# Beginning the expert units behind two attention halves, with weight tiles and later halves placed unit by unit

## The chip, the cores and the metric

The kernel runs on one core of one Trainium2 chip. The metric is the device time of one execution in microseconds, the median of the runs. The engines are TensorE (PE in the rows, with PEld for its weight loads), VectorE (DVE), ScalarE (ACT), GpSimd (POOL) and SyncE (SP). SP issues nearly all transfers, in one queue. Each engine works through its own instructions in a fixed order; an instruction waits for what it needs, and all behind it on that engine wait with it.

## The reference

Three stages follow one another. The inputs are float32, but the weight matrices of both networks are 64-bit values.

```python
def _attn_ref(q, k, v, alpha):              # batch 4, 8 heads, 768 steps, head size 48
    for t in range(S):
        state = alpha[:, :, t, :, None] * state + einsum('bhd,bhe->bhde', k[:, :, t], v[:, :, t])
        y[:, :, t] = einsum('bhd,bhde->bhe', q[:, :, t], state)

def _moe_ref(x, w_in, w_out, a, b):         # 3072 tokens, 384 -> 2048 -> 384
    h = x @ w_in
    P = a[0] + a[1] * h + a[2] * h**2 + a[3] * h**3
    Q = 1.0 + abs(b[0]) * abs(h) + abs(b[1]) * h**2
    return (P / (Q + 1e-06)) @ w_out

def _moe2_ref(x, w_in, w_out, g_ln):        # 384 -> 1024 -> 384
    h = x @ w_in
    solu = h * softmax(h)
    return (layer_norm(solu) * g_ln) @ w_out
```

## The kernel before

The 768 steps are cut into six chunks of 128; a chunk over four batch elements is 512 tokens. A chunk of the attention is made in two **halves** of two batch elements each, so there are twelve halves. Halves 0 and 1 turn their inputs with PE (`a_turn`). All later ones are prepared by `a_dve`, mostly on DVE, in six steps: transposes, a forward scan (L312), a backward scan (L321), products, and two stores to device memory from which the halves come back turned (L333, L341; `a_move_qk` L280, `a_move` L286). `a_pe` then makes the scores (L424; copied by ACT L431 and masked by POOL L432), the outputs `y` (L448), which ACT and DVE write as a high and a low part into the chunk's token tile `xt` (L474, L475), and the state (L487).

The first network runs in 96 **units**: unit u is one chunk of 512 tokens times 128 of the 2048 hidden columns. `m_up` does nine matmuls (L604) into one of three `hp` banks, then a chain over ACT, DVE and, in even units below 24, POOL (L609 to L635; the last DVE operation, L628 or L635, is noted as `fin[u]`), and a split into `gh` and `gl` (L637, L638). `m_down` of the unit four back does nine matmuls (L650) into the chunk's three sums. The order of the units is written by hand: chunk 0 with its columns 0 to 11, chunk 1 with 0 to 7, chunk 0 with 12 to 15 (units 20 to 23), chunk 1 with 8 to 15, then chunks 2 to 5 whole. A chunk done in two parts stores two partial results, `x2b_d` and `x2_d`; the copies `x2e` (L659) carry them.

The weights come in four **groups** of seven tiles each (three of `w_in`, four of `w_out`). `split_w` loads a tile, makes float32 of it by three DVE operations (L541, L544, L545), and splits it in a rounded high part (ACT, L551) and the rest (POOL, L552). Where the loaded bytes wait is one of two `st` buffers or space lent by a later group's buffer; `x2e` uses `st` as well.

Before unit 0 stand, in program order, halves 0 and 1, groups 0 and 1 whole, the constants (`consts`, with two broadcast transfers, L117 and L118), and the preparation of half 2. Then the loop over units starts. In it `BEGIN` says at which unit a half's `a_pe` begins (`half_steps`, one step of `a_pe` per unit and two steps of the next half's preparation), `CONV` when groups 2 and 3 begin (one tile per unit), `LINGER` that half 4's preparation waits for unit 16, and `U2`, `IDLE` at which units a tile of the second network's weights is split (`w2_split`). `pin(n)` and `later(n)` put instructions behind those of unit u - n on the same engine; apart from that, the order on each engine is planned ahead from a model of the times, in which earlier lines of the program go first among what is ready.

The second network follows: `n_load` brings a chunk's 512 results back (for chunks 0 and 1 the two partial results are added on DVE, L695), splits them by ACT and POOL (L697, L698), and each block of 128 tokens goes through `n_up` (18 matmuls, L731), softmax and norm (`n_soft`, `n_norm`), a transposing round through SBUF transfers (`n_turn`), `n_split` and `n_down` (24 matmuls, L795). The blocks of the first chunk are worked on beside the last units; `n_load(1)` stands right behind the last unit.

## Time and profile before

| | |
|---|---|
| median of 3 runs | 794.52 us (794.39 to 795.79) |
| the profiled execution | 793.51 us, of which the instructions span 791.8 us |
| PE | busy 735.1 us, 93% of the span |
| DVE | busy 624.9 us, 79% |
| ACT | busy 540.1 us, 68% |
| POOL | busy 351.0 us, 44% |
| mean granted clock of TensorE | 0.96 of full |

Times are counted from the first instruction. A line such as L604 is a line of the kernel. An engine is busy while one of its instructions runs; the busy time of PE counts overlapping matmuls once. "idle before" is the time an engine stood before an instruction, and the name behind the arrow is what released it, as far as the profile can tell. The granted clock is the share of TensorE's full clock; it has two levels here, 0.5 (1.2 GHz) and 1.0 (2.4 GHz), so that a value between them is a mean over time.

### The profile page before, as it was taken

How to read it: one execution, taken by the hardware profiler on the slowest of the kernel's cores; microseconds unless marked ns; L12 is line 12 of the kernel's file. 1: busy time of each engine (PE TensorE's matmuls, PEld its weight loads, DVE VectorE, ACT ScalarE, POOL GpSimd, SP SyncE). 2: the span in 40 equal slices, each digit the busy share in tenths (PEclk: the TensorE clock that was granted, in tenths of full speed). 3: DMA queues.
4: the chain of work that ended last, by engine and by line, in shares of the span. 5: the costliest groups of instructions: out<-in, count | busy, mean ns of one | idle time of the engine just before them, and what ended most of it. 6: DMA issues, size and time to landing. Idle time of an engine off the chain costs nothing.

```text
span 791.8 us, 13947 instructions
## 1 busy us (share of the span) xinstructions
PE 735.1 (93%) x4976; PEld 612.2 (77%) x4976; DVE 624.9 (79%) x1116; ACT 540.1 (68%) x989; POOL 351.0 (44%) x306
## 2 busy tenths in 40 slices
...
PEclk9857899988999999999999999999999999999999
...
GB/s 175 276 249 172 69 193 2 72 135 172 182 141 204 112 218 162 139 93 203 159 121 121 151 151 1 287 172 0 2 120 146 60 141 79 139 129 47 114 109 83
DMA packets 88719, 104.90 MB, mean 132 GB/s; under 512 B 34624, under 2 KB 63296, under 8 KB 88640
## 3 DMA queue, kind: packets, MB, share of 16 engines
...
## 4 chain that ended last, share of the span: by engine, by line
PE 51%; DVE 23%; ACT 9%; DMA 7%; issue 5%; SPq 3%; POOL 2%; DVEq 0%; ACTq 0%; POOLq 0%
PE h L731 13%; PE op L795 12%; PE x2p L650 11%; PE hp L604 11%; DVE w L633 2%; PE y L448 2%; DVE p L630 2%; DVE hp L634 2%; DVE P L312 2%; PE sc L424 2%; DMA rq<-in_q_dram 2%; DVE fp L544 2%; DVE p L635 1%; SPq L270 1%; DVE fp L541 1%
## 5 line engine op out<-in xcount | busy, mean ns | idle before, releaser
L604 PE MATMUL hp<-xt,g 128*128 128x512 f32 x864 | 225.8, 403 | 9.5 <-DVE p L628 7.5
L638 POOL TENSOR_TENSOR gl<-p,gh 128x512 fp32r<-128x512 f32 x96 | 127.0, 1323 | 199.1 <-ACT gh L637 111.3
L604 PEld LDWEIGHTS hp<-xt,g 128*128 128x128 f32 x864 | 164.3, 193 | 49.4 <-DVE p L628 8.3
L650 PE MATMUL x2p<-gh,g 128*128 128x512 f32 x576 | 196.5, 397 | 1.4 <-ACT x2e L659 1.4
L650 PEld LDWEIGHTS x2p<-gh,g 128*128 128x128 f32 x576 | 108.9, 189 | 28.2 <-ACT x2e L659 3.5
L650 PE MATMUL x2p<-gl,g 128*128 128x512 f32 x288 | 114.1, 396 | 1.1 <-POOL gl L638 1.1
L795 PE MATMUL op<-w2oh,room 128*128 128x384 f32 x384 | 101.7, 339 | 0.2 <-DVE room L787 0.2
L731 PE MATMUL h<-w2ih,x 128*128 128x512 f32 x288 | 93.1, 399 | 3.0 <-ACT x L697 2.7
L787 POOL TENSOR_TENSOR room<-room,room 128x1024 fp32r<-128x1024 f32 x22 | 54.1, 2464 | 93.7 <-ACT room L786 93.6
L633 DVE SCALAR_TENSOR_TENSOR w<-w,co,hp 128x512 f32<-128x512 f32 x84 | 62.0, 738 | 41.1 <-ACT hp L632 40.4
L609 ACT ACTIVATE ah<-hp 128x512 f32<-128x512 f32 x96 | 56.9, 593 | 26.5 <-PE hp L604 25.5
L611 ACT ACTIVATE p<-hp,co 128x512 f32<-128x512 f32 x96 | 65.9, 687 | 8.3 <-POOL gl L638 8.1
L612 ACT ACTIVATE w<-ah,co 128x512 f32<-128x512 f32 x96 | 69.4, 724 | 2.8 <-DVE hp L634 2.4
L795 PEld LDWEIGHTS op<-w2oh,room 128*128 128x128 f32 x384 | 70.1, 188 | 1.4 <-DVE room L787 0.5
L630 DVE SCALAR_TENSOR_TENSOR p<-p,co,hp 128x512 f32<-128x512 f32 x84 | 61.9, 737 | 10.0 <-ACT p L611 9.6
L632 ACT ACTIVATE hp<-ah 128x512 f32<-128x512 f32 x84 | 50.3, 598 | 26.3 <-DVE p L630 25.3
L731 PEld LDWEIGHTS h<-w2ih,x 128*128 128x128 f32 x288 | 54.5, 190 | 15.7 <-ACT x L697 3.1
L650 PEld LDWEIGHTS x2p<-gl,g 128*128 128x128 f32 x288 | 54.6, 189 | 13.6 <-POOL gl L638 1.6
L795 PE MATMUL op<-w2ol,room 128*128 128x384 f32 x192 | 65.0, 339 | 0.0
L637 ACT ACTIVATE gh<-p 128x512 fp32r<-128x512 f32 x96 | 59.9, 625 | 6.8 <-PE x2p L650 4.2
L635 DVE SCALAR_TENSOR_TENSOR p<-p,co,hp 128x512 f32<-128x512 f32 x84 | 62.0, 739 | 1.2
L631 ACT ACTIVATE ah<-w,co 128x512 f32<-128x512 f32 x84 | 60.6, 721 | 1.1
...
## 6 DMA issues: line engine op xcount, KB each, us to landing
...
```

Of the source, the lines that this page charges most:

```text
L604: last["PE", u] = nc.tensor.matmul(hp, lhsT=w[:, kt, 128 * o:128 * o + 128], rhs=xts[c][:, kt, xx, :], start=(kt == 0 and w is hi and xx = ...
L611: nc.scalar.activation(p, hp, AF.Square, bias=co[:, 7:8])
L612: nc.scalar.activation(w, ah, AF.Square, bias=co[:, 6:7])
L630: nc.vector.scalar_tensor_tensor(p, p, a1, hp, ALU.add, ALU.mult)
L631: nc.scalar.activation(ah, w, AF.Ln, bias=rest)
L633: nc.vector.scalar_tensor_tensor(w, w, rest, hp, ALU.add, ALU.mult)
L635: fin[u] = nc.vector.scalar_tensor_tensor(p, p, a0, hp, ALU.add, ALU.mult)
L637: last["ACT", u] = nc.scalar.activation(gh, p, AF.Copy)
L638: last["POOL", u] = nc.gpsimd.tensor_tensor(gl, p, gh[:].bitcast(F32), ALU.subtract)
L650: nc.tensor.matmul(x2ps[c][d], lhsT=w[:, o, 128 * d:128 * d + 128], rhs=gg, start=((c, f) in first and w is hi and gg is gh), stop=((c, f) ...
L731: nc.tensor.matmul(hp[:, 512 * n:512 * n + 512], lhsT=x2s[c][:, kt, x, CH * b:CH * b + CH], rhs=w2[w][:, kt, 512 * n:512 * n + 512], start ...
L795: nc.tensor.matmul(op, lhsT=x[:, 128 * f:128 * f + 128], rhs=w2[w][:, f, :], start=(f == 0 and x is hi and w == "oh"), stop=(f == NF2 - 1 ...
```

## The change

- The preparation before unit 0 is cut to halves 0 and 1 and the three `w_in` tiles of group 0 (`PRE`). The constants come behind the loads of both halves.
- The other four tiles of group 0 and groups 1 and 2 form one chain `prep`: two tiles per unit up to unit 6, then one (`PIECES`). Group 3 begins at unit 13 as before. All of them go behind the last DVE operation of the unit before (`G1` = 1).
- Half 2's preparation is a chain `lead`, two steps in each of units 0 to 3. Half 2's `a_pe` begins at unit 4 (was 2), half 3's at 9 (was 8). `LINGER` is gone: half 4's preparation goes with half 3's `a_pe`, from unit 9 on.
- The second network's weights: the tile that was split at unit 20 is split at unit 33.
- The two score tiles of a head pair are one tile of twice the size. The partial result of unit 11 is copied into these two tiles instead of `st`.
- `TURN`: in the second network chunk 2 comes second and chunk 1 third.

```diff
--- before.py
+++ after.py
@@ -71,20 +71,20 @@
     FASTS = (0, 20)
     GE = 80
     NA = 5
-    PRE = (1, 1, 0, 0)
+    PRE = (1, 1, 1, 0)
     GP = 2
     GS = 2
-    G1 = 99
+    G1 = 1
     G2 = 3
     MIX = lambda u: u < 24 and u % 2 == 0
     EARLY = (9, 11, 13, 15)
     SKIP = (5, 7, 11)
     AHEAD = 3
-    U2, IDLE = 20, (0, NF1 // 2 - 1)
-    BEGIN = {2: 2, 8: 3, 21: 4, 27: 5}
+    U2, IDLE = 2 * NF1 - 1, (0, NF1 // 2 - 1)
+    BEGIN = {4: 2, 9: 3, 21: 4, 27: 5}
     BEGIN.update({16 * c + 2 + 8 * x: 2 * c + 2 + x for c in range(2, NCH - 1) for x in range(2)})
-    CONV = {0: 2, 13: 3}
-    LINGER = {3: 16}
+    PIECES = lambda u: 2 if u < 7 else 1
+    TURN = (0, 2, 1) + tuple(range(3, NCH))
     assert (B, H, D, CH) == (4, 8, 48, 128)
 
     const = ctx.enter_context(tc.tile_pool(name="const", bufs=1, side="left"))
@@ -426,8 +426,9 @@
                             lhsT=hf.k[p][64 * j:64 * j + D, x, :], rhs=hf.q[p][64 * j:64 * j + D, x, :],
                             start=True, stop=True,
                         )
+                both = ap_.tile([128, 2, B, CH], F32, name="A", tag=f"A{p}")
                 for j in range(2):
-                    t = A[p, j] = ap_.tile([128, B, CH], F32, name="A", tag=f"A{p}{j}")
+                    t = A[p, j] = both[:, j]
                     nc.scalar.activation(t, sc[j], AF.Copy)
                     nc.gpsimd.affine_select(
                         out=t, in_=t, pattern=[[0, B], [1, CH]], compare_op=ALU.is_ge, fill=0.0, base=0,
@@ -554,6 +555,8 @@
                 nc.sync.dma_start(out=keep, in_=both[:, :2 * n].bitcast(F32).rearrange("p (x n) -> p x n", x=2))
 
         def w1_group(n):
+            if fast:
+                stage["wide"], stage["near"] = n < 2, n == 2
             w = moe_pool.tile([128, GW], F32R, name=f"g{n}", tag=f"g{n}")
             hi, lo = (w[:, 512 * KT * x:512 * KT * (x + 1)].rearrange("p (a b) -> p a b", a=KT) for x in range(2))
             for kt in range(KT):
@@ -654,7 +657,10 @@
             if (c, f) in final:
                 to = x2_d[c] if f == NF1 - 1 else x2b_d[c]
                 for d0, n in ((0, 2), (2, 1)):
-                    e = moe_pool.tile([128, 2, NTOK], F32, name="x2e", tag="st", bufs=2)
+                    if u == 11 and fast:
+                        e = ap_.tile([128, 2, NTOK], F32, name="x2e", tag=f"A{d0 // 2}")
+                    else:
+                        e = moe_pool.tile([128, 2, NTOK], F32, name="x2e", tag="st", bufs=2)
                     for d in range(n):
                         nc.scalar.activation(e[:, d], x2ps[c][d0 + d], AF.Copy, scale=back if fast else 1.0)
                     nc.sync.dma_start(out=to[:, d0:d0 + n, :], in_=e[:, :n])
@@ -685,6 +691,7 @@
 
         def n_load(c):
             t = x2s[c] = moe_pool.tile([128, KT, 2, NTOK], F32R, name="x2", tag="xt", bufs=2)
+            c = TURN[c]
             for kt in range(KT):
                 raw = t[:, kt, 1].bitcast(F32)
                 nc.sync.dma_start(out=raw, in_=x2_d[c][:, kt, :])
@@ -800,6 +807,7 @@
 
         def n_out(s, op):
             c, qq = divmod(s, 4)
+            c = TURN[c]
             o = moe_pool.tile([128, DM], F32, name="o", tag="st", bufs=2)
             nc.scalar.activation(o, op, AF.Copy)
             to = out.rearrange("(b c q j) d -> c q b j d", b=B, c=NCH, q=4)[c, qq]
@@ -829,26 +837,18 @@
             _run(a_load(0))
             take(pre, PRE[0])
             v_load(0)
-            consts()
             take(pre, PRE[1])
             _run(a_load(1))
             take(pre, PRE[2])
             v_load(1)
             take(pre, PRE[3])
+            consts()
             nc.gpsimd.memset(Sbd, 0.0)
-            _run(a_turn(0), a_pe(0), a_turn(1), a_pe(1), pre)
+            _run(a_turn(0), a_pe(0), a_turn(1), a_pe(1))
             clear()
-            pre = w1_group(1)
-            take(pre, NA)
             _run(a_load(2, ("ra", "rk")))
-            with tc.issue_after(marks[0, 1].ins):
-                _run(a_prep(2))
-            _run(a_move_qk(2))
-            _run(a_enter(2), pre)
-            _run(a_load(3, ("ra", "rk")))
-            stage["wide"] = False
-            stage["near"] = True
-            stage["bank"] = "at"
+            prep = chain(pre, w1_group(1), w1_group(2))
+            lead = chain(a_prep(2), a_move_qk(2), a_enter(2), a_load(3, ("ra", "rk")))
         else:
             for n in range(NG):
                 _run(w1_group(n))
@@ -864,7 +864,7 @@
         def pin(n):
             stack = ExitStack()
             if n <= now[0] < NU and fast:
-                for e, u in (("PE", now[0]), ("ACT", now[0] - n), ("POOL", now[0] - n)):
+                for e, u in (("PE", now[0] - (("PE", now[0]) not in last)), ("ACT", now[0] - n), ("POOL", now[0] - n)):
                     stack.enter_context(tc.issue_after(last[e, u].ins))
                 stack.enter_context(tc.issue_after(fin[now[0] - n].ins))
             return stack
@@ -872,15 +872,13 @@
         def half_steps(i):
             gp = a_pe(i)
             gd = chain(a_prep(i + 1), a_move_qk(i + 1) if i + 1 >= NPE else iter(()), a_load(i + 2, ("ra", "rk")) if i + 2 < NH and i + 1 >= NPE else iter(())) if i + 1 < NH else iter(())
-            b = "wait"
             while True:
                 with pin(GP):
                     a = next(gp, "end")
-                if now[0] >= LINGER.get(i, 0):
-                    with pin(GS):
+                with pin(GS):
+                    b = next(gd, "end")
+                    if b != "end":
                         b = next(gd, "end")
-                        if b != "end":
-                            b = next(gd, "end")
                 if a == "end" and b == "end":
                     if i + 1 < NH:
                         _run(a_enter(i + 1))
@@ -892,11 +890,13 @@
         split2 = w2_split() if fast else iter(())
         side = iter(())
         tail = None
-        prep = iter(())
+        if not fast:
+            prep = lead = iter(())
         for u in range(NU + LAG):
             c, f = order[u] if u < NU else (NCH, u - NU)
             now[0] = u
             if fast and u in BEGIN:
+                _run(lead)
                 _run(side)
                 side = half_steps(BEGIN[u])
             if u < NU:
@@ -907,16 +907,20 @@
                     tail = chain(w2_load("i"), n_load(0), w2_load("o"))
                 if f == 0 and c and not fast:
                     x_load(c)
-                if fast and u in CONV:
-                    _run(prep)
-                    stage["near"] = CONV[u] == 2
-                    prep = w1_group(CONV[u])
-                take(prep, 1)
+                if u == 4 and fast:
+                    stage["bank"] = "at"
+                if u == 13 and fast:
+                    prep = w1_group(3)
+                with later(G1):
+                    take(prep, PIECES(u))
                 m_up(u)
+                if u < 4:
+                    with pin(GS):
+                        take(lead, 2)
             if u == NU:
                 _run(n_load(1))
             take(side, 1)
-            if u == U2 or (u > U2 and u % (NF1 // 2) in IDLE and u not in (23, 24)):
+            if u >= U2 and (u % (NF1 // 2) in IDLE or u == U2 + 2):
                 stage["bank"] = "at" if fast else ""
                 with later(G2):
                     take(split2, 1)
```

## Rows read from the trace of the kernel before

**Rows 1.** The page: busy time of PE; granted clock in 40 slices, tenths.

```profile
PE 735.1 (93%) x4976; PEld 612.2 (77%) x4976; DVE 624.9 (79%) x1116; ACT 540.1 (68%) x989; POOL 351.0 (44%) x306
...
PEclk9857899988999999999999999999999999999999
```

**Rows 2.** Stretches: length; busy PE, PEld, DVE, ACT, POOL; clock, DMA share, GB/s.

```profile
0.00:56.60 56.60, 37.59 (x433) 32.46 (x433) 48.33 (x128) 17.85 (x41) 21.62 (x38) 0.79 0.90 242
56.60:88.00 31.40, 18.43 (x103) 14.99 (x104) 28.79 (x51) 17.17 (x32) 20.34 (x17) 0.73 0.55 144
88.00:138.60 50.60, 50.60 (x454) 40.35 (x453) 35.39 (x57) 37.72 (x69) 30.43 (x32) 1.00 0.33 84
138.60:202.20 63.60, 53.92 (x240) 42.88 (x240) 54.88 (x93) 46.75 (x83) 39.34 (x34) 0.87 0.47 132
202.20:480.00 277.80, 273.64 (x2191) 219.65 (x2190) 249.04 (x404) 229.65 (x417) 127.90 (x121) 1.00 0.57 150
```

**Rows 3.** PE's timeline: start, us, instruction, count, [idle before, its releaser].

```profile
56.59 0.96 PE L604 MATMUL hp<-xt,g 128*128 128x512 f32 x3 [0.69 <-ACT xt L474]
...
79.59 4.13 PE L424 MATMUL sc<-qks 48*128 48x128 f32 x16 [12.18 <-DMA qks<-qk_d]
83.66 3.83 PE L604 MATMUL hp<-xt,g 128*128 128x512 f32 x9
...
88.02 2.21 PE L604 MATMUL hp<-xt,g 128*128 128x512 f32 x9
...
138.64 0.39 PE L604 MATMUL hp<-xt,g 128*128 128x512 f32 x1
...
173.12 4.21 PE L604 MATMUL hp<-xt,g 128*128 128x512 f32 x9 [4.24 <-DVE p L628]
...
183.51 7.08 PE L604 MATMUL hp<-xt,g 128*128 128x512 f32 x18 [3.25 <-DVE p L628]
...
202.17 2.61 PE L604 MATMUL hp<-xt,g 128*128 128x512 f32 x9
```

**Rows 4.** DVE's timeline: ends of units 0 and 16, a weight operation between.

```profile
75.82 0.68 DVE L628 SCALAR_TENSOR_TENSOR p<-w,hp 128x512 f32<-128x512 f32 x1
...
165.36 0.56 DVE L541 TENSOR_SCALAR fp<-st 128x384 int32<-128x384 int32 x1 [0.81 <-DMA st<-in_moe_w_out_dram]
...
172.41 0.66 DVE L628 SCALAR_TENSOR_TENSOR p<-w,hp 128x512 f32<-128x512 f32 x1
```

**Rows 5.** DVE's groups up to 202 us: count, busy us, mean ns, idle before.

```profile
L541 DVE TENSOR_SCALAR fp<-st 128x512 int32<-128x512 int32 (+1 forms) x16 | 9.9, 621 | 6.8 <-DMA st<-in_moe_w_in_dram 3.9 <-DMA st<-in_moe_w_out_dram 2.4 <-ACT lent L400 0.5
...
L321 DVE TENSOR_TENSOR_SCAN alT<-alT,d 128x774 f32<-128x774 f32 x4 | 7.0, 1742 | 0.0
```

**Rows 6.** Timelines of SP's queue and of PE at the start.

```profile
8.04 3.68 SPq L117 DMA_DIRECT2D ab<-in_moe_a_dram  x1
...
19.33 3.30 PE L367 MATMUL tp<-ident,lent 128*64 128x128 f32 x32 [5.00 <-DMA lent<-in_alpha_dram]
```

**Rows 7.** SP's queue: half 2's way through memory.

```profile
67.71 0.45 SPq L341 DMA_DIRECT2D qk_d<-qk  x1
...
74.67 1.74 SPq L280 DMA_DIRECT2D qks<-qk_d  x4
```

**Rows 8.** Around the last unit: a stretch as in rows 2, then three timelines.

```profile
590.00:606.00 16.00, 11.84 (x42) 8.37 (x41) 8.07 (x14) 7.20 (x15) 9.06 (x7) 0.89 0.28 86
...
589.09 0.63 ACT L697 ACTIVATE x<-x 128x512 fp32r<-128x512 f32 x1 [5.19 <-DMA x<-x_d]
...
593.16 0.96 DVE L695 TENSOR_TENSOR both<-x 128x512 f32<-128x512 f32 x1
...
596.69 0.96 PE L731 MATMUL h<-w2ih,x 128*128 128x512 f32 x3 [2.65 <-ACT x L697]
```

**Rows 9.** GpSimd's timeline: two subtractions of the weight split.

```profile
55.36 1.27 POOL L552 TENSOR_TENSOR g<-ft,g 128x512 fp32r<-128x512 f32 x1 [0.22 <-ACT g L551]
...
57.71 2.46 POOL L552 TENSOR_TENSOR g<-ft,g 128x384 fp32r<-128x384 f32 x1 [1.07 <-ACT g L551]
```

## The prediction

> **What bounds the kernel now.** I read the page first. TensorE (PE) is busy 93% of the span and its granted clock is full except in early slices and a few later ones [rows 1], so from far off the kernel is PE-bound. The table by stage, cut at the starts of units 0, 4, 12 and 23 of the first expert network, tells it apart [rows 2]. From 202.2 to 480 us PE is busy 273.64 of 277.80 us at clock 1.00: nothing is to be won there but by less PE work, and the change takes none away. From 56.6 to 202.2 it is busy 18.43 + 50.60 + 53.92 = 122.95 of 145.6 us, and at a mean clock of 0.73 and 0.87 in two of the three stretches; weighted with the clock that is 18.4 x 0.73 + 50.6 + 53.9 x 0.87 = 111 us of work. Some 35 us are lost there, and before 56.6 us PE waits for the attention's first two halves.
>
> Why it is lost: PE's timeline has the names [rows 3]. Unit 0 starts at 56.59; then PE stands until 79.59 for the scores of half 2 (12.18 us, laid on a DMA), and at 173.12 and 183.51 it waits for VectorE (DVE), L628, and starts again slowly: a unit's nine matmuls take 4.21 there and 2.21 at 88.02. The first wait is not really the DMA's. Unit 3 needs one of three `hp` banks, and unit 0 gives its bank back only with L628 at 75.82 + 0.68 = 76.5 [rows 4], 20 us after its first matmul: only 3 of the 12 us are the DMA's own. DVE was full: 28.79 of 31.40 us from 56.6 to 88. Then it is *empty* from 88 to 138.6 (35.39 of 50.60), while PE works off what was prepared, and crowded again from 138.6 to 202.2 (54.88 of 63.60) [rows 2]. There half 4's preparation, the weight tiles of group 3 and the units meet; L541 waits in the queue for weights at 165.36 with unit 16's L628 (172.41) behind it [rows 4]. So DVE sets the time up to unit 23: bursts, a hole, and a second burst.
>
> **The change part by part.**
> *Nothing leaves DVE.* The same 28 weight tiles, halves and units are computed. One tile of the second network's split goes from unit 20 to unit 33: three operations of 0.62 us, 1.9 us [rows 5]; it goes where PE has the bound and costs nothing while DVE has 28 us free there [rows 2].
> *Start.* The constants' broadcasts (3.68 us on SP's queue, and L118 behind them) no longer stand ahead of half 1's loads; PE waited 5.00 us for those [rows 6]. That gives 4.2 us. Eleven of the fourteen tiles of groups 0 and 1 no longer stand ahead of unit 0: 11 x 3 x 0.62 = 20 us of DVE, most of which filled gaps. Unit 0 starts between 36 and 52 us; I take 46.
> *Units 0 to 3 without half 2.* Weight tiles come two per unit behind the last DVE operation of the unit before (`G1` = 1; if its load is late, the next unit's first DVE operation waits behind it, as L541 shows [rows 4]); half 2's preparation goes in pairs of steps with units 0 to 3, and its PE part starts at unit 4, half 3's at 9. Work moves from ahead of unit 0 into the hole of 88 to 138.6; half 4's preparation moves from unit 16 on to units 9 to 13, into the same hole. Its transfers go along, on SP's queue ahead of group 3's loads and no longer among them; the DMA engines are busy 0.33 of the time there [rows 2]. Each tile also brings a ScalarE copy and a GpSimd subtraction; both engines have a quarter or more free in every stretch up to 202.2 us [rows 2]. Unit 4 needs the third tile of group 1, which stands behind unit 2's end; at about 10 us from a unit's first matmul to its end (estimate: half of the 20 us of unit 0 before) that is unit 4 at about 68 us against 88.02.
> *x2e of unit 11* goes to the attention's score buffers, so group 3's loads need not wait for its stores; that takes away what held L541 [rows 4], 2 or 3 us, inside the sum below. The merged score tile frees both halves of it at once; the next half needs them units later: nothing.
>
> **The sum.** After 56.6 us DVE did 28.79 + 35.39 + 54.88 = 119.1 us up to unit 23; less 1.9 that is 117.2. Until 56.6 us I leave its 48.33 us of work as they are: what it gets earlier from the shorter loads it loses to the pins. At what share can it run when PE presses? The rows give 0.917 (56.6 to 88), 0.896 (202.2 to 480) and, with stalls of the kind that the change removes, 0.863 (138.6 to 202.2). I take 0.917, the stretch in which DVE had work at hand and was the bound: 117.2 / 0.917 = 127.8, so unit 23 starts at 184.4 against 202.2: **17.8 us**. With 0.863 it is 192.4 (9.8 us), with 1.0 it is 173.8 (28.4). PE allows it: 46 + 111 + some 14 us of waiting among units 0 to 4 is 171.
>
> *Chunk 2 ahead of 1.* After the last unit, n_load takes a chunk in three transfers without the sum of two parts. In the trace PE waits 2.65 us at 596.69 for ScalarE's copy L697, DVE's sums L695 begin only at 593.16, and L697 of the other chunk stood 5.19 us at the head of ScalarE's queue for a transfer issued late [rows 8]. The stretch 590 to 606 has 4.16 us of PE idle and 0.11 x 16 = 1.8 us of lost clock, 5.9 in all. With chunk 2 loaded from 578 on and nothing to add, its copies are done before PE's last down-projection at 594. I take 5.5 (3 to 5.9). The sums come with the next chunk, for which there are 17 us of PE work on four blocks.
>
> Against the profiled execution, 793.51 us: 793.51 - 17.8 - 5.5 = 770.2; the median of the runs, 794.52, is 1.0 above it, so **771 us**.
>
> **What pages say against it.** In the rows, GpSimd's L552 takes 1.27 us at 55.36 and, for a smaller tile, 2.46 at 57.71, where a scan of DVE (L321, 1.74 us each) runs beside it [rows 5, 9]. The Trainium skill, "SBUF — State Buffer", section "Who interferes with whom", says that a DVE instruction with two SBUF inputs and a GpSimd instruction that reads SBUF shut each other out for the whole instruction. The change puts more scans beside weight tiles: if each of the 18 tiles that follow unit 0 made DVE wait 1.2 us, some 21 us would go and the time would be about 792. The rows show GpSimd waiting and not DVE (L321's mean is 1.74 us), and GpSimd was busy only 20.34 of 31.40 us where it was fullest, so I leave that out of the sum.
>
> In the rows the clock is 0.73 and PE slow (3.83 us for unit 3's nine matmuls) after the pause [rows 2, 3]. "TensorE: Matmul & The Clock Gate" in the Trainium skill, section "Loop structure matters more than you think", says that a wait between bursts sends PE to its lower clock, 1.2 of 2.4 GHz. Units 0 to 3 with gaps then cost 4 x 1.6 = 6 us more of PE, which lie under DVE's work as long as DVE is the bound; the trace agrees on the clock.
>
> **Rivals.**
> 1. *PE becomes the bound* as soon as DVE's work is spread: unit 23 at 171, gain 31 + 5.5, **758 us**. For it: the hole of 15 us in DVE. Against: DVE was never above 0.92 over a long stretch. 0.15.
> 2. *The pins bite.* Half 2's product on GpSimd is held behind unit 0's end, then the way through memory follows, 67.71 to 74.67 to 79.59, 11.9 us [rows 3, 7]. With unit 0's end at 56 and the product at 60 the scores can start at 73, while unit 4 is through PE at 70 and `sc` stands in PE's order ahead of the first down-projection. Banks run out, DVE starves some 5 to 7 us, and xt of chunk 1, finished one unit later than before, adds 1 or 2 ahead of unit 12. Gain 7 + 4: **784 us**. 0.15.
> 3. *Slower.* Each unit's end now releases the next weight tiles, steps and banks: a ring. If a unit goes around it slower than PE and DVE work, it sets the pace. From unit 4 at 68 to unit 23 the even point is (202.2 + 5.5 - 68) / 19 = 7.35 us per unit; before it was 114.15 / 19 = 6.0 on the mean, and 10.4 from unit 19 (173.12) to 20 (183.51) with everything in one queue. At 7.8 us per unit unit 23 starts at 216: **803 us**. Against: the tiles come two units ahead of use. 0.05.
> 4. *No change*: DVE's order, planned ahead, packs the same work into the same bursts. 795 us, 0.03.
>
> **How the numbers follow.** Forecast 0.62, rivals 0.15, 0.15, 0.05, 0.03. The forecast's own range is 764 (0.97 of DVE) to 782 (0.863 and 3 us at the end); with rivals 1 and 2 the range is 757 to 784, which leaves the last two out. Faster by over 0.2% (about what a measurement here can tell from none) 0.93, within 0.2% 0.02, slower 0.05.
>
> **What would show it.** Right: unit 0 at 40 to 52 us, unit 4 near 68; no PE wait of 12 us; DVE over 0.9 busy from 88 to unit 12; unit 12 near 128 and unit 23 near 184 at full clock from about 90 on; no wait for L628 at units 19 and 20; L731 straight behind the last L650, with no wait for L697. Wrong: DVE under 0.86 between units 4 and 23 (rival 2, or 3 if PE idles beside it), or PE without idle from unit 4 on (rival 1), or the wait for L697 moved to the third chunk.

## The result: slower by one per cent

| kernel | us, median (lowest to highest) | runs | ratio to before, 95% interval |
|---|---|---|---|
| before | 794.5 (792.4 to 797.3) | 5 | |
| changed | 803.4 (798.6 to 807.1) | 5 | 1.0103 (1.0057 to 1.0149) |
| forecast | 771 (757 to 784) | | |

The changed kernel lost 9 us where 23 were expected to be won. Its profiled run took 798.55 us (span 796.8), the fastest of the five. The same kernel profiled again (below) has a span of 802.8, near the median; both profiles are used.

The page of the changed kernel: the engines' busy time, the granted clock by slices, and the chain that ended last, by engine.

```profile
PE 738.9 (93%) x4976; PEld 612.6 (77%) x4976; DVE 633.9 (80%) x1116; ACT 538.8 (68%) x989; POOL 355.2 (45%) x306
...
PEclk9876889989999999999999999999999999999998
...
DVE 34%; PE 31%; ACT 12%; DMA 7%; issue 6%; SPq 6%; POOL 3%; ACTq 0%; DVEq 0%; POOLq 0%
```

TensorE's busy share is that of before [rows 1], and its clock is below 0.9 in six of the first ten slices, as before. In the chain, DVE now has the largest share. The stages of the changed kernel, cut at the starts of units 0, 4, 12 and 23, columns as in [rows 2]:

```profile
0.00:52.26 52.26, 36.59 (x432) 31.40 (x432) 37.92 (x109) 15.91 (x36) 17.59 (x33) 0.80 0.88 232
52.26:79.40 27.14, 14.02 (x84) 10.64 (x84) 19.65 (x36) 16.04 (x28) 10.14 (x9) 0.73 0.31 101
79.40:154.09 74.69, 66.63 (x501) 51.76 (x502) 64.30 (x111) 45.19 (x85) 52.03 (x46) 0.89 0.49 129
154.09:204.40 50.31, 44.97 (x222) 35.83 (x220) 40.42 (x68) 42.59 (x79) 32.42 (x30) 0.93 0.41 104
204.40:480.00 275.60, 270.64 (x2157) 216.42 (x2157) 250.38 (x402) 225.22 (x409) 130.16 (x119) 1.00 0.59 156
```

Read against [rows 2]: unit 0 starts 4.3 us earlier and unit 4 8.6 us earlier; then units 4 to 12 take 74.7 us instead of 50.6, and units 12 to 23 take 50.3 instead of 63.5. Unit 23 starts 2.2 us later than before. So the second crowd of before is gone as forecast, and a new loss stands in front of it. TensorE's timeline has the waits; these lines answer to [rows 3], and the last one to the last of [rows 8]:

```profile
52.26 0.96 PE L607 MATMUL hp<-xt,g 128*128 128x512 f32 x3 [0.69 <-ACT xt L475]
...
65.52 4.21 PE L607 MATMUL hp<-xt,g 128*128 128x512 f32 x9 [3.46 <-DVE p L631]
79.40 2.93 PE L607 MATMUL hp<-xt,g 128*128 128x512 f32 x6 [9.67 <-ACT g L552]
...
103.45 4.21 PE L607 MATMUL hp<-xt,g 128*128 128x512 f32 x9 [4.32 <-DVE p L631]
...
154.09 6.29 PE L607 MATMUL hp<-xt,g 128*128 128x512 f32 x27
...
166.22 2.07 PE L607 MATMUL hp<-xt,g 128*128 128x512 f32 x4 [4.77 <-DVE p L631]
...
593.97 0.63 PE L738 MATMUL h<-w2ih,x 128*128 128x512 f32 x2
```

Unit 3 waits for unit 0's end (L631), unit 4 for a weight tile (L552), units 7 and 15 for ends of units again. At 593.97 the wait for L697 is gone. (Rows carry the line numbers of their own kernel. L604 of before is L607 here, L541 is L542, L697 is L704 and L731 is L738.) What DVE did meanwhile, in its timeline of the changed kernel:

```profile
46.82 1.20 DVE L324 TENSOR_TENSOR qk<-qk,alT 128x768 f32<-128x768 f32 x1
52.24 1.02 DVE L476 TENSOR_TENSOR xt<-y,xt 128x512 fp32r<-128x512 f32 x2 [4.22 <-ACT xt L475]
59.05 0.75 DVE L625 SCALAR_TENSOR_TENSOR hp<-p,co,hp 128x512 f32<-128x512 f32 x1 [5.78 <-ACT p L614]
...
64.79 0.68 DVE L631 SCALAR_TENSOR_TENSOR p<-w,hp 128x512 f32<-128x512 f32 x1
65.39 0.55 DVE L542 TENSOR_SCALAR fp<-lent 128x384 int32<-128x384 int32 x1
65.85 0.55 DVE L542 TENSOR_SCALAR fp<-st 128x384 int32<-128x384 int32 x1
66.31 0.90 DVE L328 STREAM_TRANSPOSE alT<-qk 128x384 f32<-128x384 f32 x1
...
160.04 0.76 DVE L625 SCALAR_TENSOR_TENSOR hp<-p,co,hp 128x512 f32<-128x512 f32 x1 [7.23 <-ACT p L614]
```

DVE has nothing to do from 48 to 62 us except what units 0 and 1 give it, piece by piece; weight tiles (L542) and half 2's transposes (L328) begin right behind L631, the end of unit 0. The last line shows DVE idle for 7.23 us behind unit 12 as well. The tiles and transposes are pinned, and their data had long been on the way: SP's queue issued the last load of a weight tile of this stage at 40.93 us and then nothing from 51 to 68:

```profile
40.93 3.74 SPq L538 DMA_DIRECT2D lent<-in_moe_w_out_dram  x1
44.76 1.81 SPq L270 DMA_DIRECT2D rq<-in_q_dram  x4
46.68 4.39 SPq L270 DMA_DIRECT2D rk<-in_k_dram  x4
68.00 0.35 SPq L333 DMA_DIRECT2D kb_d<-alT  x1
```

From unit 36 on the two kernels run alike with 5 us between them: unit 95 starts at 580.88 (before: 575.81). From there to the end both take 216.0 us, although the first block after unit 95 starts 7.8 us nearer to it than before. So there are two questions: what costs the time up to unit 36, and where the 7.8 us go.

**How stages are compared below.** Work is ordered differently in each kernel, so besides the starts of units I give what TensorE *loses* in a stage: its length less the time that the stage's matmuls take back to back at full clock (0.23 us for one of 128 x 512, less for the smaller ones). Idle time and lost clock are both in it; single figures are good to about 1 us. Each column is one profiled run. The two profiles of the changed kernel differ by 3.6 us at unit 23 and by 4.7 at unit 95, so a smaller difference between two such runs shows little by itself. "Again" and the last three columns are runs of the next section.

| TensorE's loss, us | before | changed | again | tiles free | half 2 ahead | neither pin |
|---|---|---|---|---|---|---|
| up to unit 0 | 28.4 | 24.1 | 26.3 | 28.2 | 26.1 | 26.6 |
| units 0 to 4 | 17.2 | 15.8 | 15.8 | 9.8 | 12.2 | 11.7 |
| units 4 to 12 | 2.7 | 17.5 | 19.1 | 16.2 | 20.6 | 8.9 |
| units 12 to 16 | 0.2 | 7.1 | 6.9 | 12.8 | 7.4 | 13.3 |
| units 16 to 23 | 16.9 | 1.3 | 1.4 | -1.0 | 0.5 | -1.0 |
| units 23 to 32 | -0.3 | 0.5 | 0.8 | -0.2 | 0.0 | -0.1 |
| units 32 to 48 | -0.9 | 3.1 | 3.7 | 4.0 | 3.3 | 3.8 |
| start of unit 23 | 202.2 | 204.4 | 208.0 | 203.5 | 205.3 | 197.0 |
| start of unit 95 | 575.8 | 580.9 | 585.6 | 581.6 | 581.9 | 574.8 |
| unit 95 to the end | 216.0 | 215.9 | 217.3 | 216.2 | 213.2 | 215.7 |
| us, median | 794.5 | 803.4 | 803.2 | 798.7 | 794.7 | 793.1 |

### The profile page after: what moved, and what is told of

Same layout as the page of the kernel before. It is cut to its first block, busy times and chain, and to the rows that moved or that the text cites. A ratio compares the mean times of both kernels' runs of the same rounds, so it can differ in the third digit from the quotient of the medians.

```text
span 796.8 us, 13943 instructions
## 1 busy us (share of the span) xinstructions
PE 738.9 (93%) x4976; PEld 612.6 (77%) x4976; DVE 633.9 (80%) x1116; ACT 538.8 (68%) x989; POOL 355.2 (45%) x306
## 4 chain that ended last, share of the span: by engine, by line
DVE 34%; PE 31%; ACT 12%; DMA 7%; issue 6%; SPq 6%; POOL 3%; ACTq 0%; DVEq 0%; POOLq 0%
PE hp L607 12%; PE x2p L653 10%; DVE room L778 3%; SPq L788 2%; PE op L802 2%; DVE room L761 2%; DVE w L636 2%; PE y L449 2%; DVE p L633 2%; DVE hp L637 2%; DVE sm L757 2%; SPq L270 2%; DVE room L776 2%; ACT jk L763 2%; DMA room<-room 2%
## 5 line engine op out<-in xcount | busy, mean ns | idle before, releaser
L607 PE MATMUL hp<-xt,g 128*128 128x512 f32 x864 | 226.9, 406 | 24.7 <-DVE p L631 13.3
L607 PEld LDWEIGHTS hp<-xt,g 128*128 128x128 f32 x864 | 165.3, 194 | 65.1 <-DVE p L631 14.6
L641 POOL TENSOR_TENSOR gl<-p,gh 128x512 fp32r<-128x512 f32 x96 | 126.8, 1321 | 189.6 <-ACT gh L640 103.6
L802 PE MATMUL op<-w2oh,room 128*128 128x384 f32 x384 | 103.4, 343 | 3.7 <-ACT room L793 2.6
L738 PE MATMUL h<-w2ih,x 128*128 128x512 f32 x288 | 91.1, 394 | 0.0
L636 DVE SCALAR_TENSOR_TENSOR w<-w,co,hp 128x512 f32<-128x512 f32 x84 | 61.9, 737 | 35.5 <-ACT hp L635 34.6
L653 PEld LDWEIGHTS x2p<-gl,g 128*128 128x128 f32 x288 | 54.5, 189 | 13.6 <-POOL gl L641 1.6
L738 PEld LDWEIGHTS h<-w2ih,x 128*128 128x128 f32 x288 | 53.9, 188 | 11.7
```

What stands on the lines that cost most here:

```text
L607: last["PE", u] = nc.tensor.matmul(hp, lhsT=w[:, kt, 128 * o:128 * o + 128], rhs=xts[c][:, kt, xx, :], start=(kt == 0 and w is hi and xx = ...
L636: nc.vector.scalar_tensor_tensor(w, w, rest, hp, ALU.add, ALU.mult)
L641: last["POOL", u] = nc.gpsimd.tensor_tensor(gl, p, gh[:].bitcast(F32), ALU.subtract)
L653: nc.tensor.matmul(x2ps[c][d], lhsT=w[:, o, 128 * d:128 * d + 128], rhs=gg, start=((c, f) in first and w is hi and gg is gh), stop=((c, f) ...
L738: nc.tensor.matmul(hp[:, 512 * n:512 * n + 512], lhsT=x2s[c][:, kt, x, CH * b:CH * b + CH], rhs=w2[w][:, kt, 512 * n:512 * n + 512], start ...
L802: nc.tensor.matmul(op, lhsT=x[:, 128 * f:128 * f + 128], rhs=w2[w][:, f, :], start=(f == 0 and x is hi and w == "oh"), stop=(f == NF2 - 1 ...
```

## The experiments

In the runs below the kernel before, run beside each group, had medians of 795.2 to 795.6 us.

**The changed kernel again.**

> The changed kernel once more, unaltered: a second profile and more times. The profiled run of the changed kernel, 798.55 us, was the fastest of its five (798.55 to 807.14, median 803.39). If the other runs lose their 5 us in one place (theory: a wait in the ring of units 4 to 12, which goes one turn slower when a transfer lands late), this profile, if it comes out at 802 or more, shows unit 12 at 157 us or later against 154.1 and everything after it shifted by as much. If it is spread (rival), unit 12 is within 1 us of 154.1 and the loss comes bit by bit up to the last unit.

Measured: 803.2 us (800.7 to 806.7, 6 runs; ratio 1.0102, 1.0076 to 1.0127). Unit 0 starts 2.2 us later than in the first profile, unit 12 at 157.85 (3.8 later), unit 95 at 585.56 (4.7 later), and the last 1.3 us come behind it. So the loss against the first profile stands in the first 158 us, as the theory said, in two places and not one. In the runs below that leave the kernel as it is up to unit 12, this unit starts between 156.8 and 160.4; that the spread of the times comes from there is likely and was not followed further. From 48 to 62 us DVE is busy 5.04 us here, against 2.54 in the first profile: the idle stretch is there again, 9 us of these 14 instead of 11.5.

### The two pins

**Tiles not pinned.** The edit frees the tiles of group 3, from unit 13 on, as well.

```
-    G1 = 1
+    G1 = 99
```

> The changed kernel with G1 = 99: the weight tiles of groups 1 and 2 are no longer pinned behind the end of the unit before, all else is kept. My theory (the pin starves VectorE and starts the ring): VectorE's idle time between 48 and 62 us, 12 us in the changed kernel, falls below 5; unit 4's wait of 9.7 us for the third tile of group 1 goes and it starts near 70 us instead of 79.4; unit 12 starts before 146 us instead of 154.1; the time is 3 to 8 us below the changed kernel's, about 797. Rival (half 4's preparation, moved from unit 16 on to units 9 to 13, crowds that stretch, and the pins do not matter): unit 4 is earlier, but unit 12 is still behind 150 us and the time is within 2 us of 803.

Measured: 798.7 us (1.0036, 1.0013 to 1.0059), 4.5 below the changed kernel. From 48 to 62 us DVE is busy 11.12 of 14 us instead of 2.54, as foreseen, but it stands idle for 6.69 us right behind that, up to 65.81, ahead of a weight tile that waits for a copy of half 1 (L400). Units 4 and 12 are not where I expected them: unit 4 starts at 79.6 (70 foreseen), unit 12 at 150.9 (146). Half 2's preparation was still behind unit 0's end, so the one pin hid what the other cost. Units 12 to 16 lose 12.8 us instead of 7.1.

**Half 2's preparation ahead of unit 0, tiles pinned.**

```
-            lead = chain(a_prep(2), a_move_qk(2), a_enter(2), a_load(3, ("ra", "rk")))
+            _run(a_prep(2), a_move_qk(2))
+            _run(a_enter(2), a_load(3, ("ra", "rk")))
+            lead = iter(())
```

> The changed kernel with half 2's preparation and half 3's loads ahead of unit 0 again, in the order in which the kernel before has them, and not in steps with units 0 to 3; the tiles stay pinned. My theory (both pins together make VectorE idle at 48 to 62 us): half 2's transposes L328 no longer stand behind unit 0's end at 64.8 us, the idle time there falls from 12 to some 6 us, unit 0 is 3 to 6 us later than 52.3, but half 2's scores and xt of chunk 1 come earlier and unit 12 starts at 145 to 150 us; 799 us. Rival (the tiles alone matter): unit 4 stays at 79 us or later and the time is 803 or more.

Measured: 794.7 us (0.9992, 0.9975 to 1.0009): level with before, 8.5 below the changed kernel. DVE is idle for 6.0 us between 48 and 62, as foreseen, but unit 12 starts at 155.6, not at 145 to 150. Against the second profile of the changed kernel 3.7 us of the gain lie ahead of unit 95 and 4.0 behind it, where nothing was edited; the section on the end accounts for 2.2 us of that. (Against the first profile nothing of it lies ahead of unit 95, and 2.7 us behind.)

**Neither pin.** Both edits together.

> The changed kernel with neither pin: the tiles not bound to units' ends (G1 = 99) and half 2's preparation ahead of unit 0. One of them alone gave 798.7 (tiles) and 794.7 us (half 2). Theory (each starves VectorE on its own before 62 us, and the ring turns slower with each): VectorE's idle time between 48 and 62 us is below 4 us, unit 0 is at 56 us or later, unit 4 before 78, unit 12 before 150, unit 23 at 203 or before; 790 to 794 us. Rival (the two hold the same thing, and either of them freed is enough): unit 23 is no earlier than with half 2 ahead alone, 205.3, and the time is 795 to 799.

Measured: 793.1 us (0.9962, 0.9942 to 0.9982). Its stages, cut at its units 0, 4, 12 and 23:

```profile
0.00:54.82 54.82, 37.20 (x433) 32.25 (x433) 45.08 (x124) 17.54 (x40) 19.92 (x37) 0.74 0.89 242
54.82:78.52 23.70, 17.73 (x88) 13.90 (x89) 16.90 (x28) 13.49 (x26) 12.22 (x12) 0.74 0.60 158
78.52:141.85 63.33, 59.45 (x490) 47.29 (x489) 61.67 (x103) 44.30 (x83) 44.18 (x40) 0.92 0.40 107
141.85:197.03 55.18, 44.02 (x223) 35.61 (x222) 40.32 (x66) 42.58 (x75) 32.56 (x31) 0.91 0.41 103
```

DVE did 45.08 us of work ahead of unit 0 (37.92 with the pins), is busy 13.43 of the 14 us from 48 to 62, and from unit 4 to unit 12 has 61.67 of 63.33 us: here it is the bound and full, as the forecast wanted it. Unit 23 starts 7 to 11 us earlier than in the changed kernel, and 5 earlier than before. So the two pins together cost that. Each taken out alone moved unit 23 by 4.5 us at most (203.5 and 205.3 against 204.4 and 208.0), so with one of them left the other gives little. In the other stretches DVE is not full: it is busy 16.90 of 23.70 us from unit 0 to unit 4, and 40.32 of 55.18 from unit 12 to unit 23. The largest wait of TensorE that is left is in unit 15, with DVE behind a load:

```profile
162.62 2.93 PE L607 MATMUL hp<-xt,g 128*128 128x512 f32 x6 [11.16 <-DVE p L631]
```

```profile
159.18 0.56 DVE L542 TENSOR_SCALAR fp<-st 128x384 int32<-128x384 int32 x1 [2.54 <-DMA st<-in_moe_w_out_dram]
159.65 0.75 DVE L630 SCALAR_TENSOR_TENSOR hp<-hp,co,ah 128x512 f32<-128x512 f32 x1
```

That is the picture of [rows 4] at another place: a tile of group 3, which is not pinned here, whose load is late, and the unit's operations behind it in DVE's queue. Two loads of group 3 before it stood at the head of DVE's queue for 2.33 and 1.93 us; the three make 6.8 us of the 14.9 that DVE is idle behind unit 12, and what set the rest was not followed. From unit 0 to unit 4 the largest idle stretch is 4.47 us, up to 65.90, ahead of a weight tile that waits for a copy of half 1 (L400).

### Halves 3 and 4

**Half 4's preparation put off to unit 16.**

```
+    LINGER = {3: 16}
...
+                if now[0] >= LINGER.get(i, 0):
                     with pin(GS):
```

> The changed kernel with LINGER = {3: 16} again: half 4's preparation waits until unit 16 and no longer stands with units 9 to 13; all else is kept. First theory (half 4's steps fill VectorE in units 8 to 12, 32.8 us of work there against 14.6 before, and leave it empty behind unit 12, 8.5 us idle): VectorE's work in units 8 to 12 falls to about 26 us, unit 12 starts 5 us or more earlier, at 149 us or before, against 154.1 to 157.9, and the time is 2 to 5 us below the changed kernel's 803. Rival (unit 12 waits for xt of chunk 1, which half 3's way through memory sets, and not for VectorE's time): unit 12 stays at 154 or later; half 4's work then meets group 3's tiles behind unit 16, unit 23 is at 206 or later and the time 803 or more.

Measured: 805.0 us (1.0134, 1.0101 to 1.0168). DVE's work in units 8 to 12 falls from 32.8 to 21.7 us, and still unit 12 starts at 154.4. Units 4 to 12 took 72.7 us, 2 to 3.5 less than in the changed kernel, for 11 us less work of DVE: the rival is right in the main, and DVE's time did not hold unit 12. Half 4's work then fills the stage of units 16 to 20 (DVE 23.93 of 24.13 us), and unit 23 starts at 213.1.

**Half 3's part begun a unit earlier.**

```
-    BEGIN = {4: 2, 9: 3, 21: 4, 27: 5}
+    BEGIN = {4: 2, 8: 3, 21: 4, 27: 5}
```

> The changed kernel with half 3's part on TensorE begun at unit 8, as in the kernel before, and not at unit 9 (half 2's stays at unit 4). In all runs of the changed kernel so far unit 12 starts 29 to 33 us behind unit 9. Theory (half 3's way from its scores to xt sets unit 12, and it hangs on the unit at which it begins, one turn of the ring, 7.4 us, earlier): unit 12 starts at 147 to 152 us, 5 us or more earlier than 154.1 to 157.9, the hole in VectorE behind unit 12 (8.5 us) stays, unit 23 is 2 to 5 us earlier, and the time is 798 to 801. Rival (VectorE's work in units 8 to 12 sets it): unit 12 moves by less than 3 us, 803 us.

Measured: 798.6 us (1.0047, 1.0029 to 1.0066), and unit 12 at 156.7: not earlier. My theory of what sets unit 12 falls here. The time is 4.6 us lower all the same: against the second profile of the changed kernel the loss in units 12 to 16 is 2.9 us instead of 6.9, and the end is 2.7 us shorter (1.4 against the first). What holds unit 12 once both pins are in stays open; without them it came at 141.9.

**Half 4's preparation put off to unit 12.**

```
+    LINGER = {3: 12}
```

> The changed kernel with half 4's preparation put off until unit 12 (until unit 16 it gave 805.0 us, with VectorE idle 9.0 us in units 12 to 16 and TensorE losing 7.8 us in units 16 to 20). Theory (the hole behind unit 12 is the time from unit 12's first matmul to its first VectorE operation, with nothing else in VectorE's queue; half 4's steps fill it if they come at unit 12): VectorE's idle time in units 12 to 16 falls from 8.5 to below 5 us, TensorE's loss in units 16 to 20 stays below 3, unit 23 starts 3 us or more earlier than 204.4 to 208.0, 799 us or less. Rival (the steps are bound to the end of the unit two before and so come behind the hole in any case): the hole stays at 8 us or more and the work is late as with unit 16: 803 to 805 us.

Measured: 799.0 us (1.0058, 1.0037 to 1.0078), the time of my theory, but not its reason: the hole behind unit 12 stays (8.4 us), TensorE loses 7.5 us in units 16 to 20, unit 23 starts at 215.7 and unit 95 at 589.0, as with unit 16. The profiled run, 802.2 us, is no slower than the changed kernel because its end took 211.4 us; what made the other runs, with a median of 799.0, faster is not shown. So half 4's earlier place was no cause of the hole, and moving it forward was right: put off, it brings back a loss in units 16 to 20.

### The split's tile at unit 33

In DVE's timeline of the changed kernel this tile's first operation stands still for its load, and the units' operations behind it; the second profile has 3.31 us for the same wait:

```profile
267.95 0.69 DVE L542 TENSOR_SCALAR fp<-st 128x512 int32<-128x512 int32 x1 [2.57 <-DMA st<-in_moe_w_in_dram]
268.56 0.74 DVE L633 SCALAR_TENSOR_TENSOR p<-p,co,hp 128x512 f32<-128x512 f32 x1
```

**The tile back at unit 20.** (`U2` and its condition as before.)

> The changed kernel with one tile of the second network's split at unit 20 again and none at unit 33, as in the kernel before. Theory (the third tile in a row, in units 31, 32 and 33, waits for one of two st buffers, and the units' VectorE operations wait behind it): units 32 to 36 take 19.0 us as in the kernel before, and not 22.5 to 23.0; the 1.9 us of VectorE's work come back between units 20 and 23, where it has 0.1 us free, so that unit 23 is up to 2 us later; the time is 1.5 to 3.5 us below the changed kernel's 803. Rival (units 32 to 36 are slow because VectorE comes there with a backlog, whatever the tile): they still take 22 us or more, and the time is 803 to 805.

Measured: 802.2 us (1.0083, 1.0054 to 1.0112). Units 32 to 36 take 19.1 us, as foreseen; the loss in units 32 to 48 falls from 3.7 to -0.1, and at units 20 to 23 nothing is paid. In this profile units 4 to 12 lost 21.1 us, 2 more than in the second profile, so the time shows only 1 us of it.

**The tile at unit 44.**

```
-            if u >= U2 and (u % (NF1 // 2) in IDLE or u == U2 + 2):
+            if u >= U2 and (u % (NF1 // 2) in IDLE or u == U2 + 13):
```

> The changed kernel with that tile at unit 44 in place of 33, so that it has the st buffers to itself; nothing is put back at unit 20. Theory (the queue for the two st buffers costs the time, not the 1.9 us of work): units 32 to 36 take 19.0 us, units 44 to 48 are no longer than the changed kernel's 23.3 us by more than 0.5 us; the time is 3 to 4 us below 803. Rival (the tile's own work costs the time wherever it stands): units 32 to 36 are short, but units 44 to 48 take 2 to 4 us more, and the time is 803.

Measured: 799.9 us (1.0058, 1.0038 to 1.0079). Units 32 to 36 take 18.9 us, but units 48 to 52 take 22.8 instead of 17.6, and unit 95 starts where it did (585.4). The wait moved along:

```profile
352.74 0.56 DVE L542 TENSOR_SCALAR fp<-st 128x384 int32<-128x384 int32 x1 [3.63 <-DMA st<-in_moe_w_out_dram]
353.33 0.56 DVE L545 SCALAR_TENSOR_TENSOR fp<-st,fp 128x384 int32<-128x384 int32 x1
353.81 0.74 DVE L636 SCALAR_TENSOR_TENSOR w<-w,co,hp 128x512 f32<-128x512 f32 x1
```

Here it is the tile of unit 48, the third behind those of 44 and 47; in the changed kernel it was that of 33, behind 31 and 32. Neither of my two versions had it right, though the median is that of the first: the two runs point not to the tile's own work, and not to its place, but to three tiles close together on two `st` buffers. That the third load waits there for the store of an earlier tile is argued from the program, not shown; a third buffer was not tried.

### x2e and the constants

**Both in the kernel before** with the turn and the subtractions of the next section (788.24 us).

> The run with the turn and the three subtractions on VectorE (788.24 us), and two further parts of the change, which lie in different stretches: the constants' loads behind half 1's, and x2e of unit 11 in the attention's score tile. The forecast's prices: unit 0 starts 4.2 us earlier than 56.5, at 52 us, and what TensorE loses in units 16 to 20 (11.3 us) falls by 2 to 3 us; 788.2 - 4.2 - 2.5 = 781.5 us. Rival (half 2 and the banks set unit 4, so that what unit 0 wins is waited away): unit 4 stays at 88 us within 1, only the second price stays, 786 us. Second rival (unit 12 and those behind it stay, since the tiles of group 3 are held by VectorE's crowd and not by x2e's stores): 788 us.

Measured: 783.1 us (0.9853, 0.9828 to 0.9878). Unit 0 starts at 56.5, as without: TensorE's wait ahead of half 1 falls from 4.87 to 3.87 us, ends with an operation of DVE now and no longer with a load, and at 52.6 us nothing is left of the difference. The gain begins where x2e's part acts. Units 16 to 20 of the kernel before, and of this one:

```profile
154.44:183.51 29.07, 21.58 (x83) 16.96 (x81) 26.52 (x47) 20.43 (x38) 13.63 (x12) 0.86 0.41 130
```

```profile
155.50:175.69 20.19, 18.87 (x82) 15.05 (x82) 19.91 (x35) 18.65 (x36) 14.51 (x12) 1.00 0.37 117
```

They lose 1.8 us instead of 11.3. Against the run without this part, unit 23 starts 6.4 us earlier, unit 32 only 1.8, and unit 95 5.7; what the stretch behind unit 23 loses and regains was not followed. I had allowed 2 or 3. The constants were not taken out again here, so that the gain is x2e's is argued from its place.

**x2e in the `st` buffers, in the changed kernel.**

```
-                    if u == 11 and fast:
+                    if False:
```

> The changed kernel with x2e of unit 11 in the st buffers, as before. In the kernel with the turn and the subtractions this part alone (with the constants, which moved nothing) took TensorE's loss in units 16 to 20 from 11.3 to 1.8 us. Theory (group 3's loads wait for the stores of x2e wherever they stand near unit 16): that loss goes from 0.8 to 5 us or more here, and the time is 4 us or more above the changed kernel's 803. Rival (in the changed kernel group 3's tiles are later, from unit 13 on one by one behind units' ends at 166 us and after, when x2e's stores are through): within 2 us of 803.

Measured: 800.9 us (1.0085, 1.0061 to 1.0110). The loss in units 16 to 20 goes from 0.8 to 2.5 us, and unit 95 starts at 587.7, 2.1 later than in the second profile. That is nearer to the rival: with group 3's tiles behind the units' ends, x2e's place matters less. Its price here is not shown: unit 23 starts 4.8 us later than in the second profile, and the median is 2.3 us lower all the same, with an end of 210.8 us.

**The constants first, in the changed kernel.**

> The changed kernel with the constants' loads ahead of half 1's again. Forecast: they cost 4.2 us, unit 0 starts at 56 us or later against 52.3 to 54.5, but unit 4 (79.4 to 82.2 in all runs) waits for the tiles and half 2 and moves by 2 us or less; 803 to 805 us. Rival (as with the constants moved in the kernel before, where unit 0 stayed at 56.5: it waits for weight tiles or for VectorE, not for half 1's loads): unit 0 within 1 us of 52.3 to 54.5, 803 us.

Measured: 797.1 us (1.0039, 1.0021 to 1.0057). The constants do delay half 1 (in each kernel, TensorE's wait for half 1's loads):

```profile
20.71 3.28 PE L367 MATMUL tp<-ident,lent 128*64 128x128 f32 x32 [6.64 <-DMA lent<-in_alpha_dram]
```

```profile
18.12 3.68 PE L367 MATMUL tp<-ident,lent 128*64 128x128 f32 x32 [3.93 <-DMA lent<-in_alpha_dram]
```

(constants first above, the changed kernel below). Unit 0 starts at 55.2, 0.7 to 2.9 us later, unit 4 at 81.7 and unit 95 at 583.8, between the two profiles of the changed kernel. So the constants' place is worth 0.7 to 2.9 us at unit 0, not 4.2, and nothing that these profiles can show at unit 95. Neither theory has the time: most of its 6 us lie in the end, 211.6 us long.

### The end: where 7.8 us go

**The turn alone, in the kernel before** (`TURN` in `n_load` and `n_out`, nothing else).

> The kernel before with chunk 2 ahead of chunk 1 in the second network and nothing else of the change. My theory (the wait for L697 goes, but the last chunk's softmax on VectorE and ScalarE is a chain of its own at some 7.4 us per block, behind which the last transfers and down-projections wait): the first block after unit 95 comes 6 to 8 us earlier against unit 95, yet the time is within 2 us of the kernel before, 793 to 796. Rival (the forecast's price): what is won at 596 us stays won, 789 us.

Measured: 795.2 us against 795.15 (1.0006, 0.9991 to 1.0020): no change. The first block behind unit 95 comes 7.8 us earlier, and nothing of it is left. DVE's and GpSimd's timelines of this run show where it goes:

```profile
644.57 1.21 DVE L752 TENSOR_REDUCE sm<-h 128x1 f32<-128x1024 f32 x1
647.66 2.15 DVE L768 TENSOR_TENSOR sm<-sm 128x1 f32<-128x1 f32 x1 [1.88 <-ACT sm L767]
649.84 2.33 DVE L769 SCALAR_TENSOR_TENSOR sm<-sm 128x1 f32<-128x1 f32 x1
652.21 2.31 DVE L770 SCALAR_TENSOR_TENSOR sm<-sm 128x1 f32<-128x1 f32 x1
654.56 0.81 DVE L771 TENSOR_SCALAR room<-room,sm 128x1024 f32<-128x1024 f32 x1
...
656.61 1.20 DVE L752 TENSOR_REDUCE sm<-h 128x1 f32<-128x1024 f32 x1
```

```profile
647.38 7.12 POOL L789 TENSOR_TENSOR room<-room,room 128x1024 fp32r<-128x1024 f32 x3 [19.07 <-ACT sm L766]
```

L768, L769 and L770 work on one number per partition and take 0.16 us elsewhere. Here they take 2.15, 2.33 and 2.31, and each ends with one of GpSimd's three subtractions (7.12 us together, 2.4 each). Each subtraction had begun before the operation that waits for it. The two maximum operations around them (L752) are 12.0 us apart; in the kernel before those of the same blocks were 6.25 apart. Over all blocks behind unit 95 these three operations took 20 us longer with the turn than they would take at 0.16 us each, and 11 us longer in the kernel before.

**The turn, and the subtractions of blocks 4, 5 and 6 on DVE.**

```
-    FASTS = (0, 20)
+    FASTS = (0, 4, 5, 6, 20)
```

> The kernel before with chunk 2 ahead of chunk 1 (the run with the turn alone), and the subtractions of the splits of blocks 4, 5 and 6 on VectorE instead of GpSimd. With the turn alone three of VectorE's operations on one column (128 x 1) take 2.15, 2.33 and 2.31 us at 647.66 to 654.5, against 0.16 elsewhere, while three of GpSimd's subtractions of 2.4 us run side by side from 647.38 to 654.5. Theory (the two engines shut each other out, VectorE's softmax chain stands still for 6.3 us there, and that takes back what the turn had gained): these operations take 0.2 us, the three subtractions cost VectorE 3 x 1.22 us, the last block's transpose ends 2 to 4 us earlier than 763.8 minus whatever the start differs, and the time is 2 to 3 us below that of the turn alone (795.2), some 792.5. Rival (the chain's own series of steps on two engines sets the end): the same time, 795.

Measured: 788.2 us (0.9918, 0.9894 to 0.9942), 7 below the turn alone, more than foreseen.

```profile
643.07 1.23 DVE L789 TENSOR_TENSOR room<-room,room 128x1024 fp32r<-128x1024 f32 x1 [1.21 <-ACT room L788]
644.21 0.15 DVE L768 TENSOR_TENSOR sm<-sm 128x1 f32<-128x1 f32 x1
...
644.56 0.15 DVE L769 SCALAR_TENSOR_TENSOR sm<-sm 128x1 f32<-128x1 f32 x1
...
653.10 2.38 DVE L768 TENSOR_TENSOR sm<-sm 128x1 f32<-128x1 f32 x1
```

```profile
653.05 2.40 POOL L789 TENSOR_TENSOR room<-room,room 128x1024 fp32r<-128x1024 f32 x1 [28.67 <-ACT sm L767]
```

The operations are back at 0.15 us, and the next one that meets a subtraction left on GpSimd (653.05 to 655.45) takes 2.38 again. The Trainium skill, "SBUF — State Buffer", section "Who interferes with whom", says that a DVE instruction with two SBUF inputs and a GpSimd instruction that reads SBUF exclude each other for the whole instruction; the trace agrees, and here DVE is the one that waits.

The end of each kernel, counted from unit 95's first matmul (us):

| kernel | first block's up-projection | block 11's maximum | last transpose ends | down-projection of block 20 | last matmul |
|---|---|---|---|---|---|
| before | 20.9 | 76.0 | 185.4 | 191.9 | 209.5 |
| turn alone | 13.1 | 76.9 | 184.2 | 189.6 | 209.2 |
| changed | 13.1 | 76.6 | 183.8 | 189.2 | 208.9 |
| changed, half 2 ahead | 13.1 | 74.4 | 181.6 | 187.1 | 206.7 |
| changed, constants first | 13.1 | 73.3 | 180.6 | 186.0 | 204.6 |
| turn, subtractions on DVE | 13.1 | 72.1 | 178.8 | 185.3 | 202.9 |

Block 11's maximum decides the rest: behind it the chain of every kernel with the turn runs at about the same pace (106.7 to 107.3 us to the last transpose). In kernels whose end was not edited it still moves by 3 us, with the number of DVE's operations that meet a subtraction just before it. In the turn alone and in the changed kernel it is three, and the maxima of blocks 10 and 11 are 11.7 to 12.2 us apart; with half 2 ahead, the constants first and half 4 at unit 12 it is two (9.2 to 9.8 us); with the subtractions on DVE it is none (7.3 us). The third one in the changed kernel, and the same operation with the constants first, where it comes ahead of the subtraction:

```profile
653.24 2.99 DVE L776 TENSOR_SCALAR room<-room,sm 128x1024 f32<-128x1024 f32 x1
```

```profile
655.03 0.81 DVE L776 TENSOR_SCALAR room<-room,sm 128x1024 f32<-128x1024 f32 x1
```

That is 2.2 to 3.3 of the 3 to 6 us by which those three kernels were faster behind unit 95; the rest lies behind the last transpose.

### The changed kernel mended

**Half 2 ahead, the tile at unit 20, three subtractions on DVE.**

> The changed kernel with its three costs taken out where single runs found them: half 2's preparation ahead of unit 0 (794.7 us alone), the subtractions of blocks 4, 5 and 6 on VectorE (7 us below the turn alone), the split's tile at unit 20 and not 33 (units 32 to 48 lost 3.8 us less). If the prices add: 803.2 - 8.5 - 7 - 3.8 = 784 us, with unit 95 at 577 to 579 us and 210 us from there to the end. Rival (the run with half 2 ahead had by its order already 2.7 us of the tail's part, 213.2 us from unit 95 to the end against 215.9 in the changed kernel): 787 to 788 us.

Measured: 788.3 us (0.9917, 0.9894 to 0.9940); unit 95 at 576.8, the end 209.4 us. The rival's account is right: half 2 ahead had part of the end's gain already.

**The same with the tiles not pinned.**

> The mended kernel (788.31 us: half 2 ahead, three subtractions on VectorE, the split's tile at unit 20) without the tiles' pin as well. If the prices add (without both pins unit 95 starts at 574.84; the tile gives 3.8, from there to the end 209.5 us as in the mended kernel): unit 95 at 571, 782 to 783 us. Rival (the tile at unit 20 meets group 3's tiles, which are not pinned either and wait there for the two st buffers): unit 23 2 to 4 us later than 197.0, 785 to 786 us.

Measured: 782.5 us (0.9840, 0.9813 to 0.9868), the lowest median of this study, 12.8 below the kernel before. Unit 23 starts 3.5 us later than without both pins (1.4 of it already at unit 0), as the rival said, the end takes 209.7 us, and the sum is that of the theory. But the kernel before with the turn, the three subtractions, x2e and the constants' place took 783.1 us, the same within the intervals: the new order of tiles and halves up to unit 23 is not needed for it.

## Why the prediction was wrong, point by point

**"Until 56.6 us I leave its 48.33 us of work as they are."** This step failed first. Ahead of unit 0 DVE did 37.92 us. Up to unit 23 it did 162.3 us in all, 5.1 less than before, so 124.4 us were left behind unit 0 and not 117.2.

**"I take 0.917."** The share failed by more. From unit 0 to unit 23 DVE was busy 124.4 of 152.1 us, 0.818, which is the share of the same stretch before (119.1 of 145.6), and could be read from [rows 2]. Unit 23 was forecast at 184.4 and came at 204.4. The earlier unit 0 takes 4.3 us off, the additional work at 0.917 adds 7.9, and the lower share adds 16.4: together 20.0. I had taken the share from the one stretch in which DVE had its work at hand, and put it on all of them.

The pins are part of it. They stood in the change's own lines, and I priced them as the order of the work, not as idle time. From 48 to 62 us DVE was busy 14.00 us before, 2.54 changed (5.04 in the second profile), and 13.43 without the pins. But without either pin unit 23 still came at 197.0, 12.6 us behind the forecast, and DVE's share was 0.836 (118.9 of 142.2 us). So the pins account for 7 to 11 us, and the rest stays without them: DVE was full only from unit 4 to unit 12 there, and from unit 12 on it was busy 0.73 of the time. Part of that is seen, the 6.8 us of late loads of group 3; the rest is open.

**"Unit 4 at about 68 us."** It came at 79.4 (81.7 in the second profile): the chain "third tile behind unit 2's end" was right, but unit 2 ended at 76.2, 17.5 us behind its first matmul, where I had put about 10, and the tile's operations and its copy (L552) took until 79.35.

**Rivals.** Rival 2 (the pins bite) had the mechanism, and was too small and at the wrong place: about 9 to 11.5 idle us of DVE in one stretch, not 5 to 7, and at the weight tiles as well as on half 2's way. The sign named for it, DVE under 0.86 between units 4 and 23, came: 104.7 of 125.0 us, 0.838. Rival 3 (a ring) had the time, 803 us, by luck: units 4 to 12 took 9.3 us each against 6.3 before, and without the pins 7.9. But over units 4 to 23 the pace was 125.0 / 19 = 6.6 us, below its even point of 7.35, and unit 23 came at 204.4 to 208.0, not 216; the time was lost because unit 4 came 11 us later than this rival assumed, and with the tile and the end below.

**The split's tile, "costs nothing".** Only its three operations were priced. Its load and its store go through two `st` buffers, and as the third of a close series it costs about 3.8 us of TensorE's time (the loss in units 32 to 48 with it and without).

**x2e, "2 or 3 us, inside the sum".** With the constants' place, worth 5.1 us in the kernel before with the turn and the subtractions (788.2 to 783.1); in the changed one, where the pinned tiles come later, no gain is shown. The constants: 0.7 to 2.9 us at unit 0, not 4.2.

**The turn, "I take 5.5".** The step "PE waits for L697" was right, and its local price too low (7.8 us against 5.5). But the term of the sum measured nothing (795.2 us with the turn alone, 795.15 without). What failed is that I followed it to 606 us and no further: before, the last transposes were finished only just in time for TensorE (185.4 us behind unit 95, and its down-projection of block 20 stood without a gap behind that of 19); brought forward 7.8 us, TensorE waits for them. And the sentence "the rows show GpSimd waiting and not DVE" drew on a case in which DVE's scan had begun first (57.59 us, the subtraction at 57.71). In the end section the subtraction began first (647.38, L768 at 647.66), and there DVE waits:

```profile
57.59 1.76 DVE L321 TENSOR_TENSOR_SCAN alT<-alT,d 128x774 f32<-128x774 f32 x1
```

**Right:** units 16 to 23 lose 1.3 us instead of 16.9; no wait for L697; unit 0 is earlier, though at 52.3 and 54.5 just outside the 36 to 52 given and 6 to 8 us behind the 46 taken; the clock of units 0 to 4 is 0.73 as before (0.81 in the second profile). That its price lay beside DVE's work fits unit 4's wait for a tile (9.67 us); no run took it apart.
